# A softcap attention and a mixture-of-experts attention in one kernel: the last pair and batch in an order of their own, logits beside q, projections in pieces, gate weights loaded first

## The chip, the cores and the metric

One core of a Trainium2 chip runs the whole program. Its engines are TensorE (PE, with its weight loads shown apart as PEld), VectorE (DVE), ScalarE (ACT), GpSimd (POOL) and SyncE (SP, which here only issues transfers). The metric is device microseconds of one execution; lower is better.

## What is computed

```python
def _attn_ref(q, k, v, cap):
    scores = scale * np.matmul(q, k.transpose(0, 1, 3, 2))
    scores = cap * np.tanh(scores / cap)
...
    return np.matmul(attn, v).astype(np.float32)

def _moe_ref(x, w_gate, wq, wk, wv, wo):
    logits = x @ w_gate
...
    for e in range(E):
        q = x @ wq[e]
        k = x @ wk[e]
        v = x @ wv[e]
        scores = scale * (q @ k.transpose(0, 2, 1))
...
        ye = a @ v @ wo[e]
        for kk in range(K):
            mask = topk[:, :, kk] == e
            out += mask[..., None] * w[:, :, kk:kk + 1] * ye
```

q, k and v have 8 batches of 12 heads with 448 rows of 64; cap is 30, and the first attention's softmax runs over the last axis. Its output, the 12 heads side by side, is the `x` of the second part (8 x 448 x 768). That has 4 experts of size 64 with causal attention (a is its softmax); each row takes the two experts with the largest logits, weighted by the softmax over these two (w).

## The kernel before

The first attention is worked off in 48 pairs of heads, six to a batch (`NP`, `HP`). For a pair p, ACT does four tanh instructions ("T", on two or one score tiles of 448 columns) and two exps ("E"); the scores come from TensorE into two PSUM tiles of two banks each (`ps_score`). The rest of a pair is casts on POOL (`a_cast`), transposes of q and k (`a_tr`, "tr"), the product with v and the division (`a_pv`, "pv", in two halves) and a transpose of the result into `xT`, the x of the batch (`a_xt`, "xt"). These use four PSUM banks, taken in turn (`ps_aux`).

When the six pairs of a batch b are done, its second part runs beside the pairs of the next batch: q and k projections for two expert pairs r (`b_q`, `b_k`), four v projections with the gate's logits as four more columns of the same matmuls (`b_v`, weights `wvg`), the gate (`b_gate`, `b_gexp`, `b_gate2`), causal scores (`b_fill`) and their exps on ACT ("X", `b_exp`) with masks on POOL, the product with v and the division by DVE (`b_pv`), a transpose (`b_ot`) and eight half-rows of output projection (`b_wo`), which go out by DMA.

`prog` is the order of ACT's work, slot by slot, written by hand; the X of batch b stand in slots 6(b+1)+3 and 6(b+1)+5 (`EXPB`). For TensorE a planner (`Plan`) keeps a clock for PE, DVE and ACT from fixed costs. Each unit of work has a cost, what it depends on, and a due time. `step` takes, among the units that could start first (within 0.05 us), the one due first; `pump` does so up to the next score fill; `force` hurries one unit and what it depends on. Every engine then executes its instructions in the order emitted.

For the last batch the q and k projections are split: `b_early` sums the first five of six steps in score banks once pair 46 is there, one unit for each of q and k and r, and `b_late` adds the sixth. After the last slot, `plan.pump` emits all the rest in the planner's order.

Weights are loaded by POOL's DMA queue (q0 in the page), three loads a slot from slot 1 on, in the order of the list `loads`: wq and wk of the four experts in turn, then the four wv, then the gate's 768 x 4, then wo (line 695 issues them). The inputs q, k, v of two pairs at a time are loaded by SP's queue, eight pairs ahead.

Of the kernel before, what the change touches and what calls it, by code (L numbers as in the profile page):

```python
# [8 lines left out]
f32 = mybir.dt.float32  # L9
# [6 lines left out]
class Plan:  # L16
# [7 lines left out]
    def __init__(self):  # L24
        self.pe = self.dve = self.act = 0.0
        self.done = {}
        self.aux = [0.0] * 4
        self.naux = 0
        self.work = []

    def ready(self, u):
# [5 lines left out]
        if u["aux"]:  # L37
            t = max(t, self.aux[self.naux % 4])
        return t

    def emit(self, u):
# [7 lines left out]
        if u["aux"]:  # L49
            self.aux[self.naux % 4] = end  # L50
            self.naux += 1
        self.done[u["key"]] = end

# [25 lines left out]
    def known(self, key):  # L79
        return key in self.done or any(u["key"] == key for u in self.work)  # L80

    def force(self, key):


        def hurry(k):
            for u in self.work:
                if u["key"] == k:
# [8 lines left out]
    def add(self, key, pe, dve, deps, due, fn, *args, aux=True):  # L96
        self.work.append(
            dict(key=key, pe=pe, dve=dve, deps=deps, aux=aux, due=due, fn=lambda: fn(*args))
        )


@with_exitstack
def kernel(
# [189 lines left out]
    pr = {}  # L293
# [18 lines left out]
    def a_pv(p, i):  # L312

        pv = ps_aux.tile([128, 2, 2, Dh + 1], f32, name=f"pv{i}_{p}", tag="aux")
        pt = (pr[(p, 0)], pr[(p, 1)])
        for n in range(2):
            w = WIN[2 * i + n]
            nc.tensor.matmul(  # L318
                pv[:, n, :, :], pt[0][:, KC, w : w + 128], vtz[p % 8], start=True, stop=False,
                skip_group_check=True,  # L320
            )
            for g in range(2):
                for c in range(KC):
                    nc.tensor.matmul(  # L324
                        pv[:, n, g, :], pt[g][:, c, w : w + 128], v16[p % 8][:, g, c, :],
                        start=False, stop=(c == KC - 1), skip_group_check=True,
                    )
# [9 lines left out]
        )  # L337

# [21 lines left out]
    def b_v(b, n):  # L360
        s = st[b]
        if n == 0:
# [4 lines left out]
        ps = ps_aux.tile([128, E * Dh + E], f32, name=f"vps_{b}_{n}", tag="aux")  # L367
        for j in range(NDC):
            nc.tensor.matmul(  # L369
                ps, xT[b][:, j, w : w + 128], wvg[:, j, :], start=(j == 0), stop=(j == NDC - 1)  # L370
            )
        pse = ps[:, 0 : E * Dh].rearrange("p (e d) -> p e d", d=Dh)
        nc.vector.tensor_copy(s["lg"][:, n, :], ps[:, E * Dh : E * Dh + E])
        if n < 3:
            evac(s["vall"][:, n, :, 0:Dh], pse, act=(b == B - 1))
# [6 lines left out]
    def b_gexp(b):  # L382
        s = st[b]
        s["eexp"] = bp.tile([128, 4, E], f32, name=f"eexp_{b}", tag="eexp")
        nc.scalar.activation(s["eexp"], s["lg"], AF.Exp)

    def b_gate(b):
# [10 lines left out]
        nc.vector.tensor_tensor(mske, lg, m1.broadcast_to(sh), ALU.is_equal)  # L398
# [5 lines left out]
        nc.vector.tensor_tensor(sel, lg, m2.broadcast_to(sh), ALU.is_ge)  # L404
# [19 lines left out]
    def b_qk(b, r, which, ps, j0, j1):  # L424
        w2 = wq2 if which == "q" else wk2
        for j in range(j0, j1):
            nc.tensor.matmul(  # L427
                ps, w2[r][:, j, :], xT[b][:, j, :], start=(j == 0), stop=(j == NDC - 1)
            )
        if j1 < NDC:  # L430
            return
        if which == "q":
            qe = bp.tile([128, S], f16, name=f"qe_{b}_{r}", tag="qe")
            evac(qe, ps, act=(b == B - 1))
            st[b]["qe", r] = qe
            return
# [4 lines left out]
        nc.vector.tensor_copy(kk[64:128, S + TL : 2 * S], ps[64:128, 0:KM])  # L441

    def b_q(b, r):
        ps = ps_aux.tile([128, S], f32, name=f"qps_{b}_{r}", tag="aux")
        b_qk(b, r, "q", ps, 0, NDC)

    def b_k(b, r):
        ps = ps_aux.tile([128, S], f32, name=f"kps_{b}_{r}", tag="aux")
# [385 lines left out]
```

## Time and profile before

| | us |
|---|---|
| median of 3 runs | 356.16 |
| lowest and highest | 352.48 and 358.13 |
| the profiled execution | 357.48 |
| its span in the profile | 355.4 |
| mean granted TensorE clock in it | 0.947 of full speed |

The profile is of one execution on the chip. Times in it are microseconds from the start of the span. A busy time is the sum of an engine's instructions, an idle time is what stood before an instruction, with what ended it after the arrow. The granted clock is 1.0 at 2.4 GHz and 0.5 at 1.2 GHz; a stage's figure is the mean over it.

### The profile page before, as it was taken

To read this page: it belongs to the slowest core of one execution; us is meant where nothing else is said; L and a number is where in the kernel's file an instruction comes from. 1 tells how busy PE (TensorE), PEld (TensorE's weight loads), DVE (VectorE), ACT (ScalarE), POOL (GpSimd) and SP (SyncE) were. 2 spreads that over 40 slices of the span, in tenths; PEclk is the share of its full clock that TensorE was granted. 3 is DMA by queue.
4 is the path that set the end of the run, shared out by engine and by line. 5 is a ranking of instruction groups with operands and counts; after the bars stand their busy time and mean duration, and the time that the engine had idled before them with its cause. 6 is when DMAs were issued, how large, how long until landed. Compare 5 with 4: busy or idle time off the path is not lost.

```text
span 355.4 us, 8921 instructions
## 1 busy us (share of the span) xinstructions
PE 291.3 (82%) x3271; PEld 194.0 (55%) x3271; DVE 251.5 (71%) x881; ACT 308.5 (87%) x340; POOL 164.9 (46%) x527
## 2 busy tenths in 40 slices
PE   4876772897899969997999889988998899896854
PEld 1454441575567556765666656756675656563531
DVE  3366552378778797889678986988688877872382
ACT  1999995499999999999999999999999999971402
POOL 3879999063914383257516480739153602021300
PEclk9599998599999999999999999999999999998678
DMA  5979999930071915374257507670621011100134
GB/s 156 281 189 251 248 227 223 226 93 3 2 243 61 281 39 163 129 222 114 71 176 234 145 9 227 190 201 3 201 92 23 2 46 76 37 2 2 44 111 156
DMA packets 65579, 46.19 MB, mean 130 GB/s; under 512 B 25920, under 2 KB 62400, under 8 KB 65536
## 3 DMA queue, kind: packets, MB, share of 16 engines
q1 hardware_dynamic: 53712, 42.84, 42.1%
q0 software_dynamic: 10512, 1.58, 6.3%
q10 hardware_dynamic: 1312, 1.21, 1.1%
q8 instruction: 25, 0.41, 0.5%
q14 instruction: 18, 0.15, 0.1%
HBM read 36.19 MB, written 11.01 MB: 133 GB/s over the span
## 4 chain that ended last, share of the span: by engine, by line
ACT 69%; DMA 10%; PE 8%; POOL 4%; DVE 3%; SPq 2%; issue 2%; ACTq 0%; POOLq 0%
ACT y L300 31%; ACT p L307 31%; ACT pB L490 7%; DMA wvg<-in_moe_w_gate_dram 4%; DMA kf<-in_k_dram 4%; DMA vf<-in_v_dram 2%; PE vps L369 2%; PE qkps L427 1%; PE wops L551 1%; PE sB L478 1%; POOL wvg L695 1%; DVE osc L528 1%; PE s L289 1%; SPq L165 1%; PE qps L427 1%
## 5 line engine op out<-in xcount | busy, mean ns | idle before, releaser
L300 ACT ACTIVATE y<-s 128x896 f16<-128x896 f32 x192 | 153.3, 885 | 9.9 <-PE s L289 9.8
L307 ACT ACTIVATE p<-y 128x1792 f16<-128x1792 f16 x96 | 150.3, 1567 | 0.0
L498 POOL TENSOR_SCALAR_AFFINE_SELECT pB<-pB 128x128 f16<-128x128 f16 (+1 forms) x128 | 31.9, 280 | 151.1 <-ACT pB L490 150.0
L289 PE MATMUL s<-qt,kz 128*128 128x448 f16 x288 | 82.0, 361 | 17.4 <-ACT y L300 10.4
L324 PE MATMUL pv<-v,p 128*128 128x65 f16 x1152 | 60.0, 194 | 2.4 <-ACT p L307 2.2
L324 PEld LDWEIGHTS <-p 128*128 128x128 f16 x1152 | 51.9, 98 | 8.6 <-ACT p L307 3.5
L289 PEld LDWEIGHTS <-kz 128*128 128x128 f16 x288 | 27.0, 99 | 30.7 <-issue 19.5
L334 DVE TENSOR_TENSOR xk<-pv,rc 128x256 f16<-128x256 f32 x96 | 40.7, 424 | 3.3
L318 PE MATMUL pv<-vtz,p 128*128 128x130 f16 x192 | 42.2, 220 | 0.3
L200 DVE COPY ob<-wops 128x384 f32<-128x384 f32 (+1 forms) x60 | 33.4, 556 | 8.9 <-PE wops L551 7.6
L490 ACT ACTIVATE pB<-sB 128x1024 f16<-128x1024 f32 (+1 forms) x32 | 31.8, 996 | 5.0 <-PE sB L478 5.0
L369 PE MATMUL vps<-wvg,xT 128*128 128x260 f16 x192 | 28.4, 286 | 7.7 <-DMA wvg<-in_moe_w_gate_dram 7.7
L200 DVE COPY kz<-tps 64x384 f16<-64x384 f16 x94 | 32.9, 350 | 0.7
L551 PE MATMUL wops<-wo,oT 128*128 128x384 f16 x128 | 31.9, 341 | 1.1 <-DVE ob L200 0.9
L218 POOL CAST q<-qf 112x512 f16<-112x512 f32 x46 | 28.2, 613 | 2.1 <-DMA qf<-in_q_dram 0.2
L266 DVE COPY qt<-tps 128x384 f16<-128x384 f16 x48 | 16.9, 352 | 16.3 <-PE tps L256 16.2
L369 PEld LDWEIGHTS <-xT 128*128 128x128 f16 x192 | 19.0, 101 | 15.2 <-issue 9.7
L219 POOL CAST k<-kf 128x384 f16<-128x384 f32 x48 | 24.5, 510 | 5.8 <-DMA kf<-in_k_dram 5.8
L235 POOL CAST v<-vf 128x384 f16<-128x384 f32 x48 | 24.3, 507 | 3.2 <-DMA vf<-in_v_dram 0.3
L240 POOL CAST vtz<-vtf 64x64 f16<-64x64 f32 x96 | 22.7, 237 | 2.9
L355 DVE COPY xT<-xtp 128x448 f16<-128x448 f16 x48 | 18.5, 385 | 7.7 <-PE xtp L344 7.3
L333 DVE RECIPROCAL rc<-pv 128x4 f32<-128x4 f32 x96 | 17.2, 179 | 8.9 <-PE pv L324 7.2
(96 smaller groups left out, 487.6 us busy)
## 6 DMA issues: line engine op xcount, KB each, us to landing
qf<-in_q_dram SPq DMA_DIRECT2D x23, 448.0 KB, 4.8
kf<-in_k_dram SPq DMA_DIRECT2D x23, 384.0 KB, 5.3
vf<-in_v_dram SPq DMA_DIRECT2D x23, 384.0 KB, 4.9
out_dram<-ob SPq DMA_DIRECT2D x21, 384.0 KB, 2.4
out_dram<-ob SPq DMA_DIRECT2D x10, 192.0 KB, 2.7
ktf<-in_k_dram SPq DMA_DIRECT2D x46, 32.0 KB, 4.6
vtf<-in_v_dram SPq DMA_DIRECT2D x46, 32.0 KB, 4.2
out_dram<-ob ACTq DMA_DIRECT2D x3, 192.0 KB, 1.9
```

The costliest lines, as they stand in the source:

```text
L200: (nc.scalar.copy if act else nc.vector.tensor_copy)(dst, src)
L218: eng.tensor_copy(q16, qf.rearrange("p h (c d) -> p c h d", c=QC))
L289: nc.tensor.matmul(sc[:, o, 0:S], lhsT, qt, start=True, stop=True)
L300: nc.scalar.activation(y[(p, g)][:, 2 * (i % 2) : 2 * (i % 2) + n, :], score.pop((p, i))[:, 0:n, 0:S], AF.Tanh, scale=isc / capf,)
L307: nc.scalar.activation(pt, y.pop((p, g)), AF.Exp, scale=capf)
L318: nc.tensor.matmul(pv[:, n, :, :], pt[0][:, KC, w : w + 128], vtz[p % 8], start=True, stop=False, skip_group_check=True,)
L324: nc.tensor.matmul(pv[:, n, g, :], pt[g][:, c, w : w + 128], v16[p % 8][:, g, c, :], start=False, stop=(c == KC - 1), skip_group_check=True,)
L334: nc.vector.tensor_tensor(xt[p][:, 2 * i : 2 * i + 2, :, :], pv[:, :, :, 0:Dh], rc.broadcast_to((128, 2, 2, Dh)), ALU.mult,)
L369: nc.tensor.matmul(ps, xT[b][:, j, w : w + 128], wvg[:, j, :], start=(j == 0), stop=(j == NDC - 1))
L490: nc.scalar.activation(pb[:, o0 : o0 + n], st[b].pop(("sc", r, g))[:, 0:n], AF.Exp, scale=isc)
L498: nc.gpsimd.affine_select(out=blk, in_=blk, compare_op=ALU.is_ge, fill=0.0, base=0, pattern=[[1, n]], channel_multiplier=-1,)
L551: nc.tensor.matmul(ps, s["oT", r][:, w : w + 128], wo2[r][:, c0:c1], start=(r == 0), stop=(r == 1))
```

## The change

- The planner can split a unit into parts (`parts`). The first part opens one of the four banks, the last closes it. q and k projections come in three parts of two matmuls, v projections in two of three, the two halves of a pair's product with v in two parts each.
- `loads` starts with the gate weights, issued in slot 0. Then come wq, wk of experts 0 and 1, the four wv, wq, wk of experts 2 and 3, and wo.
- Batch 6's second X pair moves from slot 47 to slot 46. Batch 7's X leave `prog`; slot 47 is four T, then the three remaining E.
- From batch 6 on, due times of the last steps are drawn together (`pace`).
- The last batch's early projections become one unit for each step j, for q and k and both r. The logits of the last batch leave the v projections; 24 matmuls of 4 columns (`b_logit`) sum them in the columns behind q in q's bank.
- `last_batch` writes the order by hand: pair 47's product, head 0 under the last exp and head 1 after it, the transposes, the remaining steps of q, k and logits, then the copies (ACT takes q and a third of k), scores, exps, gate, v projections between the scores, products, and an output projection whose first half (r = 0) for two row blocks is summed before the second product is ready. Three of four output blocks go out as one transfer each.

```diff
@@ class Plan
+    def parts(self, key, n, pe, dve, deps, due, fn, *args):
+        for i in range(n):
+            d = deps if i == 0 else [(*key, "part", i - 1)]
+            aux = "open" if i == 0 else "close" if i == n - 1 else None
+            self.add(
+                (*key, "part", i), pe / n, dve * (i == n - 1), d, due, fn, *args, i, aux=aux,
+                group=key,
+            )
...
+    def b_logit(j0, j1):
+        for j in range(j0, j1):
+            for n in range(4):
+                nc.tensor.matmul(
+                    early[0][:, 0, S + E * n : S + E * (n + 1)],
+                    xT[B - 1][:, j, WIN[n] : WIN[n] + 128], wvg[:, j, E * Dh : E * Dh + E],
+                    start=False, stop=(j == NDC - 1), skip_group_check=True,
+                )
...
-    loads = []
-    for e in range(E):
-        cols = slice(e % 2 * Dh, (e % 2 + 1) * Dh)
-        loads += [(wq2[e // 2][:, :, cols], rows(moe_wq[e]))]
-        loads += [(wk2[e // 2][:, :, cols], rows(moe_wk[e]))]
-    for e in range(E):
-        loads += [(wvg[:, :, e * Dh : (e + 1) * Dh], rows(moe_wv[e]))]
-    loads += [(wvg[:, :, E * Dh : E * Dh + E], rows(moe_w_gate))]
+    loads = [(wvg[:, :, E * Dh : E * Dh + E], rows(moe_w_gate))]
+    for r in range(2):
+        for e in (2 * r, 2 * r + 1):
+            cols = slice(e % 2 * Dh, (e % 2 + 1) * Dh)
+            loads += [(wq2[r][:, :, cols], rows(moe_wq[e])), (wk2[r][:, :, cols], rows(moe_wk[e]))]
+        if r == 0:
+            for e in range(E):
+                loads += [(wvg[:, :, e * Dh : (e + 1) * Dh], rows(moe_wv[e]))]
...
-    EXPB = {HP * (b + 1) + 3 + 2 * r: (b, r) for b in range(B) for r in range(2)}
+    EXPB = {HP * (b + 1) + 3 + 2 * r - (b == B - 2) * r: (b, r) for b in range(B - 1) for r in range(2)}
...
+            prog += t + e1 + [("S", NP), ("E", p, 0), ("E", p, 1)]
...
-        for _ in range(3 if p else 0):
+        for _ in range(3 if p else 1):
...
+            plan.parts(("q", b, r), 3, 1.13, 0.55, [x], t - 4.0, b_qk, b, r, "q")
+            plan.parts(("k", b, r), 3, 1.13, 0.75, [x], t - 4.0, b_qk, b, r, "k")
...
+            plan.parts(("v", b, n), 2, 0.66, 0.6, d, t0 + 2.0 * n, b_v, b, n)
...
+    def last_batch():
...
+        for i in range(2):
+            for n in range(2):
+                do(plan.done["E", p, 0], 0.18, a_pv_mm, p, i, n, (0,))
+        at = [0.0, 0.0]
+        for i in range(2):
+            for n in range(2):
+                at[i] = do(plan.done["E", p, 1], 0.13, a_pv_mm, p, i, n, (1,)) + 0.6
+            a_pv_out(p, i)
...
+        t = do(at[1] + 0.2, 0.22, a_xt, p) + 0.35
+        for r in range(2):
+            for w in "qk":
+                plan.force(("e", r, w, NDC - 2))
+        plan.force(("el", NDC - 2))
...
+        for r in range(2):
+            for w in "qk":
+                t = do(t, 0.19, b_qk_mm, b, r, w, ps[r, w], NDC - 1, NDC)
+            if r == 0:
+                t0 = do(t, 0.18, b_logit, NDC - 1, NDC)
+        for r in range(2):
+            b_q_out(b, r, ps[r, "q"], True)
+            b_k_out(b, r, ps[r, "k"], True)
+            if r == 0:
+                for i in range(2):
+                    do(0.0, 0.33, b_v, b, 0, i)
+                b_gexp(b, lgp)
+                nc.vector.tensor_copy(s["lg"], lgp)
+        for g in range(2):
+            t = do(t0 + 1.1, 0.43, b_fill, b, 0, g)
+            b_exp(b, 0, g)
+        b_gate(b)
+        b_gate2(b)
+        for i in range(2):
+            do(0.0, 0.33, b_v, b, 1, i)
+        t = do(t + 0.4, 0.43, b_fill, b, 1, 0)
+        b_exp(b, 1, 0)
...
+        t = do(t, 0.46, b_pv, b, 0)
+        t = do(t + 0.3, 0.46, b_pv, b, 1) + 0.8
+        do(t, 0.22, b_ot, b, 0)
...
+        b_pv(b, 2)
+        wo(0, (0,))
+        b_pv(b, 3)
+        wo(1, (0,))
+        plan.pump(1.0e9, 1.0e9)
+        b_ot(b, 1)
+        for n in range(2):
+            wo(n, (1,))
+        for n in range(2, 4):
+            wo(n, (0, 1))
```

## Rows read from the trace of the kernel before

**Rows 1.** The page's first part: busy us, share of the span, instructions.

```profile
PE 291.3 (82%) x3271; PEld 194.0 (55%) x3271; DVE 251.5 (71%) x881; ACT 308.5 (87%) x340; POOL 164.9 (46%) x527
```

**Rows 2.** Stages: length, busy time of five engines, granted clock, DMA share, GB/s.

```profile
55.00:75.00 20.00, 11.96 (x112) 8.05 (x109) 7.70 (x27) 10.37 (x12) 8.25 (x28) 0.74 1.00 221
75.00:317.85 242.85, 216.05 (x2616) 149.55 (x2615) 198.45 (x695) 242.85 (x265) 108.34 (x351) 1.00 0.36 109
317.85:326.50 8.65, 6.51 (x58) 3.62 (x57) 3.46 (x9) 0.53 (x1) 0.00 (x0) 0.94 0.01 2
326.50:334.00 7.50, 4.84 (x19) 2.45 (x19) 1.32 (x3) 4.28 (x5) 2.75 (x12) 0.50 0.00 0
```

**Rows 3.** Waits: engine, tile and line, whom for; total us, times, longest.

```profile
ACT y L300 <- PE s L289: 9.8, 4, 7.4
```

**Rows 4.** Timeline, ACT, 57 to 72 us: start, length, instruction, idle before.

```profile
65.48 0.54 ACT L300 ACTIVATE y<-s 128x448 f16<-128x448 f32 x1 [7.35 <-PE s L289]
...
69.62 1.73 ACT L300 ACTIVATE y<-s 128x896 f16<-128x896 f32 x2 [2.02 <-PE s L289]
71.61 1.02 ACT L490 ACTIVATE pB<-sB 128x1024 f16<-128x1024 f32 x1 [0.26 <-PE sB L478]
```

**Rows 5.** Timeline of TensorE's matmuls over the same stretch.

```profile
55.35 0.54 PE L289 MATMUL s<-qt,kz 128*128 128x448 f16 x2 [0.22 <-ACT y L300]
63.61 1.46 PE L369 MATMUL vps<-wvg,xT 128*128 128x260 f16 x6 [7.72 <-DMA wvg<-in_moe_w_gate_dram]
...
66.46 2.44 PE L427 MATMUL qps<-xT,wq 128*128 128x448 f16 x6
```

**Rows 6.** DMA issues of places 11, 12, 13: KB each, us to landing.

```profile
wvg<-in_moe_wv_dram POOLq DMA_DIRECT2D x1, 96.0 KB, 12.6
wvg<-in_moe_wv_dram POOLq DMA_DIRECT2D x1, 96.0 KB, 15.3
wvg<-in_moe_w_gate_dram POOLq DMA_DIRECT2D x1, 6.0 KB, 14.5
```

**Rows 7.** Timeline, POOL: issues of places 10 to 12, then 13.

```profile
43.95 2.46 POOL L695 DMA_DIRECT2D wvg<-in_moe_wv_dram  x3
...
48.98 0.83 POOL L695 DMA_DIRECT2D wvg<-in_moe_w_gate_dram  x1
```

**Rows 8.** The page's DMA queues: POOL's, with packets, MB, share.

```profile
q0 software_dynamic: 10512, 1.58, 6.3%
```

**Rows 9.** The chain that ended last, from 317 us on: start, length, what.

```profile
317.79 0.95 PE qkps L427 x5
...
321.63 0.22 PE xtp L344 x4
...
323.02 0.54 ACT qe L200
...
323.99 0.62 DVE kzB L439
...
324.85 0.49 DVE kzB L441
...
326.51 1.03 ACT pB L490
...
332.85 1.30 PE vps L369 x6
...
336.25 0.67 PE vps L369 x6
...
338.79 0.56 DVE ob L200
...
342.05 0.20 DVE rcB L525
...
342.47 0.42 DVE osc L528
...
347.00 2.43 PE wops L551 x7
```

More of the change, by code (lines that the diff above doesn't have):

```diff
@@ L28, in __init__ @@
         self.naux = 0
+        self.opened = {}
         self.work = []
@@ L36, in ready @@
             t = max(t, self.done[d])
-        if u["aux"]:
+        if u["aux"] in ("open", "whole"):
             t = max(t, self.aux[self.naux % 4])
@@ L48, in emit @@
             end = self.dve + self.LAT
-        if u["aux"]:
-            self.aux[self.naux % 4] = end
+        if u["aux"] in ("open", "whole"):
+            slot = self.naux % 4
             self.naux += 1
+            self.aux[slot] = end
+            if u["aux"] == "open":
+                self.aux[slot] = 1.0e9
+                self.opened[u["group"]] = slot
         self.done[u["key"]] = end
+        if u["aux"] == "close":
+            self.aux[self.opened.pop(u["group"])] = end
+            self.done[u["group"]] = end
     def step(self, until, latest):
@@ L79, in known @@
     def known(self, key):
-        return key in self.done or any(u["key"] == key for u in self.work)
+        return key in self.done or any(key in (u["key"], u["group"]) for u in self.work)
     def force(self, key):
@@ L310, with a_pv_mm, a_pv_out @@
     xt = {}
[L312 to L327, printed above, removed]
+    pvs = {}
+    def a_pv_mm(p, i, n, heads):
+        if n == 0 and 0 in heads:
+            pvs[p, i] = ps_aux.tile([128, 2, 2, Dh + 1], f32, name=f"pv{i}_{p}", tag="aux")
+        pv = pvs[p, i]
+        w = WIN[2 * i + n]
+        for g in heads:
+            pt = pr[(p, g)]
+            if g == 0:
+                nc.tensor.matmul(
+                    pv[:, n, :, :], pt[:, KC, w : w + 128], vtz[p % 8], start=(n == 0),
+                    stop=False, skip_group_check=True,
+                )
+            for c in range(KC):
+                nc.tensor.matmul(
+                    pv[:, n, g, :], pt[:, c, w : w + 128], v16[p % 8][:, g, c, :],
+                    start=False, stop=(c == KC - 1), skip_group_check=True,
+                )
+    def a_pv_out(p, i):
+        pv = pvs.pop((p, i))
         if i == 0:
@@ L539, in b_ot, with b_wo_mm, b_out @@
         s["oT", r] = oT
+    def b_wo_mm(b, n, f, ps, rs):
+        w = WIN[n]
+        for r in rs:
+            nc.tensor.matmul(
+                ps, st[b]["oT", r][:, w : w + 128], wo2[r][:, f * (D // 2) : (f + 1) * (D // 2)],
+                start=(r == 0), stop=(r == 1),
+            )
     def b_wo(b, n, f):
         s = st[b]
-        w = WIN[n]
-        lo = 64 if n == 3 else 0
-        c0, c1 = f * (D // 2), (f + 1) * (D // 2)
         if f == 0:
             s["ob"] = outp.tile([128, D], f32, name=f"ob_{b}_{n}", tag="ob")
-        ob = s["ob"]
         ps = ps_aux.tile([128, D // 2], f32, name=f"wops_{b}_{n}_{f}", tag="aux")
-        for r in range(2):
-            nc.tensor.matmul(
-                ps, s["oT", r][:, w : w + 128], wo2[r][:, c0:c1], start=(r == 0), stop=(r == 1)
-            )
+        b_wo_mm(b, n, f, ps, (0, 1))
+        b_out(b, n, f, ps)
+    def b_out(b, n, f, ps):
+        lo = 64 if n == 3 else 0
+        w = WIN[n]
+        c0, c1 = f * (D // 2), (f + 1) * (D // 2)
+        ob = st[b]["ob"]
         last = b == B - 1
         evac(ob[lo:128, c0:c1], ps[lo:128, :], act=last and f == 1)
-        if last:
+        if last and n == 3:
             eng = nc.sync if f == 0 else nc.scalar
```

195 lines of the change are left out of this document (114 added, 81 removed).

## Prediction

> **What bounds the kernel now.** I read the page's first part first, to see which engine can set the time: ACT is busy 87% of the span, and no other engine over 82% [rows 1]. An average says little here, so the stages came next. Between 75.00 and 317.85 us ACT is busy for 242.85 of 242.85 us [rows 2]: the middle of the kernel is a string of tanh and exp without a gap, and nothing that only rearranges other engines can shorten it. What can be won lies in two places: the 20 us before 75.00, of which ACT works 10.37, and the 37.55 us after 317.85, where the attention pairs are over and the last batch drains.
>
> The list of waits names the first place: ACT waited for TensorE's scores, 9.8 us in 4 waits, the longest 7.4 [rows 3]. In order of time, ACT sits idle 7.35, 2.02 and 0.26 us, 9.63 in all, between 58.1 (65.48 less 7.35) and 71.6 [rows 4]. TensorE's side shows why: the scores at 55.35 are followed by nothing until the first v projection of batch 0 starts at 63.61, after 7.72 us of waiting for the gate weights [rows 5]. TensorE takes its work in order, so the scores behind that projection wait too. Its first work after the hole is slow: six q matmuls take 2.44 us, against 0.95 for five late in the kernel [rows 5, 9]. The granted clock over the stage is 0.74, a mixture of both levels, after an engine that stood still for over 7 us [rows 2]. Part of the second idle time, 2.02 us, is this.
>
> The chain of work from 317 us on shows the second place [rows 9]. The last exp of pair 47 ends at 317.85 [rows 2], the first exp of batch 7 starts at 326.51, the first division of its attention at 342.05, its last output projection at 347.00, and the span ends at 355.40. That is 8.66 + 15.54 + 4.95 + 8.40 = 37.55 us of one thing after another.
>
> **The change, step by step: gate weights first.** Before, POOL issues the gate load at 48.98 as the 13th of 17 [rows 7] and it lands 14.5 us later, at 63.5, where TensorE goes on [rows 6, 5]. After, it is issued right after pair 4's casts, near 24, and batch 0 needs it at about 55.9: far ahead. What is late next? The wv loads move from places 9 to 12 of the big loads to 5 to 8, so they land before 50. But wq and wk of experts 2 and 3 now take places 9 to 12. The loads that held places 11 and 12 were issued at about 44.8 and 45.6 and took 12.6 and 15.3 us [rows 6, 7], landing at 57.4 and 60.9. POOL issues each 0.83 us later, since the gate load's own 0.83 us [rows 7] now lies ahead of them: 58.2 and 61.7. The first is wq of expert 3, the second wk of expert 3. TensorE wants q of the second expert pair right behind the first v projection: in the old order only one score tile, two sets of transposes and then that q stand there [rows 5], so at about 57 without the hole. ACT has work until 58.1 [rows 4], so a wait until 58.2 costs it under a microsecond. The k of that pair stood behind the v projections before. As smaller pieces it can slip between them, and would then wait up to 61.7. I take 2.1 us of ACT idle time for both together and a gain of 7.5. The bounds are 9.63 (no wait) and 3.0 (TensorE blocked from 57 to 61.7, and then as much recovery as the 2.3 us seen now, which makes near 7 lost).
>
> **Projections in pieces, weights' order, one exp pair moved.** Cutting q, k, v and the attention products into pieces adds no matmul; it lets the planner fill smaller gaps. In the middle this is worth nothing, because ACT has no idle time there [rows 2]. The cover is ACT itself; if a piece opened a bank and blocked TensorE, ACT would lose it directly (a rival, below). Batch 6's second expert pair moves one slot earlier, out of the last one. It is the same ACT work, but the last slot then has four tanhs in a row with no exp between, so the third must wait for scores whose bank is released one tanh earlier. I put 0.5 us on that, between 0 and one score fill with its latencies, about 1.
>
> **From the last exp to the first exp of batch 7 (8.66 us).** Now four runs of five early projections stand in TensorE's order behind the last exp, 0.95 us each [rows 9]. After, single steps are emitted as soon as each transposed pair is there, so most of this runs during the last slot, and half of pair 47's product runs under the last exp. I build the path: 0.6 for the second half of the product, 1.3 for two divisions (0.20 and 0.42 each, by the like operations of [rows 9], with latencies), 0.8 for four transposes and their copy (0.22 and 0.4): the last projection step starts at 2.7 after the exp, and ACT's copy of q at 3.1, which now starts at 323.02, 5.2 after it. Now k is projected only after that copy, and then three DVE copies follow, from 323.99 to 325.34 [rows 9]. After, k follows q at once, and ACT takes the third copy: k is ready at about 4.1 instead of 7.5. Then a cost that the change adds: the logits share q's bank, so the bank is free for the scores only when the logits are copied out, and that copy stands on DVE behind the first v evacuation: I put that at 5.1. Scores at full clock 0.5: first exp at 5.7, saving 2.9. The logits' own 24 matmuls of 4 columns, no dearer than the 0.055 us of a transpose (four in 0.22 [rows 9]), are 1.3 us, five sixths of it before the path.
>
> **From the first exp to the first division (15.54 us).** Now a second late projection, four v projections, batch 6's output projections and the nine gate operations stand in one line. Six v matmuls cost 1.30 us at clock 0.5 and 0.67 at full clock [rows 9]; the stage's first half ran at 0.50 [rows 2]. After, both projections come ahead of the scores, the gate runs on DVE under the exps, and the v projections stand between score fills. What stays is ACT: four exps of about 0.95 [rows 9] and two copies of at most 0.5, some 4.5 to 4.8, and about 1.0 for the last v copy and the first product. I take 5.5, saving 10.0. If TensorE ran at the low level throughout, three v's and three fills would add some 3 us.
>
> **The rest.** The division-to-output stage keeps its order of divisions, and its first transposes hold up the next products: 5.2 against 4.95. Behind it, half of the output sums are made beforehand, and three outputs go as one transfer each instead of two: 7.5 against 8.40, most of it copies and the transfer's landing, which don't shrink. Sum 5.7 + 5.5 + 5.2 + 7.5 = 23.9. Against it stand leftovers of batch 6: eight output copies of 0.56 on DVE [rows 9], which ran in the tail before and, as TensorE was already 89% busy in the middle [rows 2] and now gets the early projections there, partly will again. Three of them on the path are 1.6: 25.5 in place of 37.55, a saving of 12.0, with bounds 7.5 (low clock and all leftovers) and 14.
>
> **Sum.** 357.48 (the profiled execution; its span is 355.4, so 2.1 lie around it) - 7.5 + 0.5 - 12.0 = 338.5. That execution stands 1.3 above the median of the runs; I say 338.
>
> **Rivals.**
> *The wait moves to the second pair's weights.* For it: their loads take the very places that landed at 57.4 and 60.9. The gate load has as many pieces as a big one: 10512 packets on that queue [rows 8] are 13 loads of 784 and 4 of 80, so it counts with 784. If pieces rather than bytes set the pace, putting it first pushes all others back by the 2.6 us by which it landed after its predecessor (63.5 less 60.9), to 60.8 and 64.3. TensorE then stalls as now, the gain is about 2.5, and the time 357.48 - 2.5 + 0.5 - 12.0 = 343.5. Against it: k stood late in the old order. The Trainium skill's page "DMA: Bandwidth & Descriptors" (Why small descriptors are slow) gives such a rule: the engine pays a fixed overhead for each packet. By it this rival is the likelier; the trace agrees in so far as 6 KB took about as long as 96 KB [rows 6].
> *The tail gives half back.* Gaps remain while DVE divides, and TensorE fell to clock 0.5 after gaps of this kind [rows 2]; with all leftovers the saving is 7: time 343.5. For it: DVE's copies of 0.56 sit between divisions now [rows 9]. Against: the new order has more to do in each gap.
> *Everything lands.* 9.63 and 14: 334.
> *Banks held open block the middle; slower than before.* An open piecewise sum holds one of four banks until its last piece is done; with two or three open, the running pair's products wait for a bank, TensorE stands, and ACT follows. DVE, which frees them, is 82% busy (198.45 of 242.85 [rows 2]). The cost falls on seven batches: at 2.8 us of ACT idle time a batch the gain of 19 is gone, at 3.8 the kernel is over 2% slower, about 365. Against: ACT has zero idle time there now with whole projections.
>
> **Chances.** Forecast 0.50; weights 0.22; tail 0.13; everything 0.07; blocked middle 0.04; smaller mishaps that leave it within 2% 0.04. About 2% is what a measurement tells from no change. Faster by over 2% holds for the first four: 0.92; within 2% 0.06; slower 0.02. The range takes the bounds: 334 for all gains less the 1.3 of the profiled execution, so 332 in round numbers, up to 347 (gains of 3.0 and 7.5); beyond it lie about 0.15.
>
> **What would show it.** The wait on the gate weights gone, ACT's idle time between 55 and 75 down from 9.6 to about 2, and what is left put down to projections of the second pair. ACT still without idle time from there to the last exp, which ends near 311. From it to the first exp of batch 7 5.7 us, to the first division 5.5 more, to the end of the span 25.5 in all, with the early projections ahead of the last exp. Wrong would be idle time on ACT in the middle, another wait of 4 us or more on a weight load near 57, or a granted clock of 0.5 through most of the last 25 us.

## The result, and the profile after

| | before | after |
|---|---|---|
| median, us | 355.24 | 340.15 |
| lowest and highest | 352.48 and 358.13 | 339.57 and 342.68 |
| the profiled execution, its span | 357.48, 355.4 | 342.68, 341.0 |
| granted clock in it | 0.947 | 0.989 |

The ratio is 0.9614, with a 95% interval of 0.9526 to 0.9702: faster, by 3.9%. It compares the means of the fast runs, 340.64 after and 354.32 before, where the run of 358.13 counts as slow and is left out. The forecast was 338 with a range of 332 to 347. The total came out close, but two of its terms did not: the tail gave 8.3 us in place of 12.0, and the head, in nine of ten traces with the new loads and pieces, gave 9.6 in place of 7.5. That they partly cancel is luck.

The page's first part, and the waits of ACT (engine, tile and line, whom for; total us, times, longest), after:

```profile
PE 280.2 (82%) x3295; PEld 190.1 (56%) x3295; DVE 251.1 (74%) x877; ACT 308.4 (90%) x341; POOL 165.2 (48%) x527
...
ACT ob L223 <- DVE ob L223: 8.2, 1, 8.2
...
ACT qe L223 <- PE qkps L506: 6.0, 1, 6.0
ACT pB L540 <- PE sB L528: 2.4, 1, 2.4
ACT y L323 <- PE s L312: 1.9, 4, 1.0
```

ACT's own work is what it was [rows 1]: 308.4 us. Only idle time around it went. The wait of 9.8 us for scores [rows 3] is down to 1.9. Of the waits left, two long ones belong to the tail: 6.0 us for the first copy of q, and 8.2 at the very end.

Stages of after: length, busy time of five engines, granted clock, DMA share, GB/s. They answer to [rows 2]:

```profile
55.00:75.00 20.00, 16.36 (x178) 11.37 (x177) 12.24 (x44) 16.18 (x18) 13.29 (x43) 0.91 0.89 205
75.00:308.00 233.00, 206.84 (x2496) 143.30 (x2496) 190.41 (x660) 233.00 (x256) 103.23 (x335) 1.00 0.39 115
```

Between 55 and 75 us ACT works 16.18 us in place of 10.37. In the middle it has no gap, either before or after. The last exp of pair 47 ends at 311.76 (307.58 and 4.18 in the row below); before, at 317.85.

The tail of after, from ACT's timeline (start, length, instruction, idle before and what ended it):

```profile
307.58 4.18 ACT L330 ACTIVATE p<-y 128x1344 f16<-128x1344 f16 x3
317.77 0.53 ACT L223 CAST qe<-qkps 128x448 f16<-128x448 f32 x1 [6.02 <-PE qkps L506]
319.23 0.47 ACT L223 CAST kzB<-qkps 64x384 f16<-64x384 f32 x1 [0.92 <-DVE kzB L483]
321.75 1.89 ACT L540 ACTIVATE pB<-sB 128x1024 f16<-128x1024 f32 x2
```

and from its chain of work (start, us, what), answering to [rows 9]:

```profile
325.84 0.20 DVE rcB L575
...
332.54 2.71 DMA out_dram<-ob
```

So the tail's stages are 9.99 us from last exp to first exp of batch 7 (311.76 to 321.75), 4.09 to the first division (325.84), and 15.16 to the end (341.0): 29.24. Before they were 8.66, 15.54 and 13.35: 37.55. The whole gain lies in the middle one; the first and the third grew.

The account of the two profiled executions: ACT's idle time from 50 to 80 us fell from 9.63 to 3.81 (5.82), the rest up to the last exp was 0.27 shorter, the tail 8.31, and what lies around the span 0.4 (2.1 against 1.7). That is 14.8, the difference of 357.48 and 342.68.

### The profile page after: what moved, and what is told of

Its sections match the earlier page's. It is cut to its first block, busy times and chain, and to the rows that moved or that the text cites. A ratio compares the mean times of both kernels' runs of the same rounds, so it can differ in the third digit from the quotient of the medians.

```text
span 341.0 us, 8954 instructions
## 1 busy us (share of the span) xinstructions
PE 280.2 (82%) x3295; PEld 190.1 (56%) x3295; DVE 251.1 (74%) x877; ACT 308.4 (90%) x341; POOL 165.2 (48%) x527
## 4 chain that ended last, share of the span: by engine, by line
ACT 85%; PE 6%; DMA 2%; issue 2%; DVE 2%; POOL 1%; ACTq 0%; POOLq 0%
ACT y L323 39%; ACT p L330 37%; ACT pB L540 7%; POOL pB L548 1%; DMA kf<-in_k_dram 1%; PE qkps L469 1%; PE vps L407 1%; PE s L312 1%; DMA out_dram<-ob 1%; PE sB L528 1%; DMA vtf<-in_v_dram 1%; DVE ob L223 1%; PE qps L469 0%; PE pv L351 0%; ACT L223 0%
## 5 line engine op out<-in xcount | busy, mean ns | idle before, releaser
L351 PE MATMUL pv<-v,p 128*128 128x65 f16 x1152 | 66.2, 194 | 1.2 <-ACT p L330 1.0
L351 PEld LDWEIGHTS <-p 128*128 128x128 f16 x1152 | 53.7, 98 | 11.0 <-ACT p L330 2.0
L312 PEld LDWEIGHTS <-kz 128*128 128x128 f16 x288 | 26.2, 98 | 26.4 <-issue 13.1
L379 PE MATMUL xtp<-perm,xk 128*128 128x128 f16 x144 | 21.0, 223 | 14.4 <-DVE xk L364 14.2
L594 PE MATMUL wops<-wo,oT 128*128 128x384 f16 x128 | 29.8, 325 | 1.7 <-DVE oT L588 1.7
L407 PE MATMUL vps<-wvg,xT 128*128 128x260 f16 (+1 forms) x192 | 30.6, 276 | 0.0
L379 PEld LDWEIGHTS <-xk 128*128 128x128 f16 x192 | 14.6, 98 | 27.3 <-DVE xk L364 19.1
L289 DVE COPY qt<-tps 128x384 f16<-128x384 f16 x48 | 16.9, 352 | 15.2 <-PE tps L279 14.8
```

Source lines behind the costliest of these rows:

```text
L312: nc.tensor.matmul(sc[:, o, 0:S], lhsT, qt, start=True, stop=True)
L351: nc.tensor.matmul(pv[:, n, g, :], pt[:, c, w : w + 128], v16[p % 8][:, g, c, :], start=False, stop=(c == KC - 1), skip_group_check=True,)
L379: nc.tensor.transpose(ps[:, 128 * n : 128 * (n + 1)], src(n), first if n < 3 else last)
L407: nc.tensor.matmul(ps, xT[b][:, j, w : w + 128], wvg[:, j, 0:cols], start=(j == 0), stop=(j == NDC - 1),)
L594: nc.tensor.matmul(ps, st[b]["oT", r][:, w : w + 128], wo2[r][:, f * (D // 2) : (f + 1) * (D // 2)], start=(r == 0), stop=(r == 1),)
```

## The experiments

One table first, from each kernel's trace, in us. "Idle" is ACT's idle time from 50 to 80 us; A is the end of the last exp of pair 47; then the way from A to ACT's first copy of q, on from there to the first exp of batch 7 (X), to the first division (D), and to the end of the span. The medians are of the timed runs, the ratios against runs of the kernel before that were timed beside them. Each trace is of one execution.

| kernel | idle | A | A to q copy | q copy to X | X to D | D to end | median | ratio and 95% interval |
|---|---|---|---|---|---|---|---|---|
| before | 9.63 | 317.85 | 5.17 | 3.49 | 15.54 | 13.35 | 355.24 | |
| after | 3.81 | 311.76 | 6.01 | 3.98 | 4.09 | 15.16 | 340.15 | 0.9614 [0.9526, 0.9702] |
| e1 | 0.70 | 309.85 | 5.16 | 3.07 | 15.22 | 13.40 | 351.82 | 0.9802 [0.9716, 0.9888] |
| e2 | 10.68 | 318.74 | 6.02 | 3.97 | 5.61 | 15.06 | 351.31 | 0.9795 [0.9716, 0.9873] |
| e3 | 0.00 | 312.43 | 6.02 | 3.97 | 5.76 | 15.12 | 343.46 | 0.9590 [0.9518, 0.9662] |
| e4 | 0.00 | 308.07 | 7.26 | 3.97 | 5.76 | 15.14 | 341.91 | 0.9636 [0.9568, 0.9704] |
| e5 | 0.00 | 308.68 | 6.24 | 3.32 | 4.08 | 15.18 | 340.41 | 0.9586 [0.9515, 0.9656] |
| e6 | 0.00 | 307.47 | 6.01 | 3.97 | 5.76 | 13.89 | 339.56 | 0.9568 [0.9493, 0.9643] |
| e7 | 0.52 | 312.15 | 6.43 | 3.97 | 4.09 | 15.16 | 348.10 | 0.9687 [0.9591, 0.9782] |
| e8 | 0.00 | 308.86 | 5.21 | 3.91 | 6.41 | 16.71 | 343.25 | 0.9681 [0.9587, 0.9776] |
| e9 | 0.00 | 308.03 | 6.32 | 3.96 | 4.10 | 16.89 | 341.49 | 0.9597 [0.9529, 0.9665] |
| e10 | 0.00 | 307.67 | 6.02 | 3.96 | 4.10 | 14.55 | 338.26 | 0.9511 [0.9449, 0.9573] |
| e11 | 0.00 | 308.81 | 6.03 | 3.97 | 4.09 | 15.20 | 340.21 | 0.9550 [0.9485, 0.9615] |
| f2 | 0.00 | 308.72 | 6.76 | 3.32 | 4.08 | 13.42 | 338.19 | 0.9498 [0.9453, 0.9542] |

### e1: the loads alone

```diff
 # kernel before
-    loads = []        # wq, wk of four experts, four wv, the gate
+    loads = [gate]    # then wq, wk of 0 and 1, four wv, wq, wk of 2 and 3
-        for _ in range(3 if p else 0):
+        for _ in range(3 if p else 1):
```

> The kernel before with the new order of weight loads alone. If the parts simply add, the head's share is what ACT's idle time between 55 and 75 us loses: from 9.6 us to about 4 to 5, so the time falls by 5 to 6, to about 350, and the 37.6 us behind the last exp stay as they were. Rival: the wait only moves to the second expert pair's weights in full, because the old order asks for that q right behind the first v projection, as one unit of six matmuls: then ACT's idle time stays at 7 or more and the time falls by under 3.

### e2: all of the change but the loads

```diff
 # kernel after
-    loads = [gate]    # the new list
+    loads = []        # the list of before
-        for _ in range(3 if p else 1):
+        for _ in range(3 if p else 0):
```

> The changed kernel with the old order of loads: the gate weights are 13th again. If the wait on them is a matter of the loads alone, TensorE stands still until they land, at about 63, some 8 to 9 us because the first v projection now comes earlier (54.3), ACT is idle some 9 to 10 us there, and the time is 5 to 6 us over that of the changed kernel, 345 to 346. Rival: the pieces make room for other work before the first v projection and soften the wait: then under 3 us over it.

The load order alone gives 2.0%, the rest alone 2.05%, and together they give 3.9%: the two gains add up as far as intervals of some 0.9% either way can tell, and neither alone is clear of 2%. In e2 the hole of [rows 5] is back, a little longer than expected (9.81 us of TensorE, 10.68 of ACT). TensorE's and ACT's timelines of e2:

```profile
64.07 0.81 PE L407 MATMUL vps<-wvg,xT 128*128 128x260 f16 x3 [9.81 <-DMA wvg<-in_moe_w_gate_dram]
...
66.84 1.36 ACT L323 ACTIVATE y<-s 128x896 f16<-128x896 f32 x2 [9.77 <-PE s L312]
```

The gate weights cause it, whatever the shape of the projections. In e1, with whole projections, the hole shrinks to one wait of TensorE, for the load that the forecast called late next. ACT's idle time falls to 0.70 us, not to the 4 to 5 expected; but the traced execution, 348.73, is the shortest of e1's four, and the others (351.42 to 354.31) are not traced.

```profile
59.91 1.30 PE L427 MATMUL qps<-xT,wq 128*128 128x448 f16 x6 [0.92 <-DMA wq<-in_moe_wq_dram]
```

### e3: four loads in slot 0

```diff
-        for _ in range(3 if p else 1):
+        for _ in range(3 if p else 4):
```

> The changed kernel with four weight loads in slot 0 instead of one, so that each load behind them is issued a slot, some 5 us, sooner. Theory: what is left of the head's wait (TensorE 2.7 us before the q of the second expert pair, ACT 3.8 us in all) ends when the wq of expert 3 lands. Then the wait and the idle time are gone and the last exp ends 3 to 4 us earlier; the time falls by 3. Rival: the queue moves at its own pace and sooner issues only wait in it: the landing moves by under 1 us, and so does the time. Second rival: POOL's 2.5 us of issuing in slot 0 delay the casts of pairs 5 and 6, and ACT waits near 30 to 45 us instead.

In after's own profile wq of expert 3 landed late. POOL issued it at 45.17 and it took 19.0 us, so it landed near 64.1; TensorE goes on at 64.22. Issues and the DMA list (last column: us to landing), then TensorE's and ACT's timelines, all of after:

```profile
23.67 0.97 POOL L746 DMA_DIRECT2D wvg<-in_moe_w_gate_dram  x1 [0.24 <-issue]
45.17 0.83 POOL L746 DMA_DIRECT2D wq<-in_moe_wq_dram  x1
...
wq<-in_moe_wq_dram POOLq DMA_DIRECT2D x1, 96.0 KB, 19.0
...
64.22 0.91 PE L469 MATMUL qps<-xT,wq 128*128 128x448 f16 x2 [2.69 <-issue]
...
65.96 0.97 ACT L540 ACTIVATE pB<-sB 128x960 f16<-128x960 f32 x1 [2.39 <-PE sB L528]
67.36 0.92 ACT L323 ACTIVATE y<-s 128x896 f16<-128x896 f32 x1 [0.42 <-PE s L312]
69.28 0.54 ACT L323 ACTIVATE y<-s 128x448 f16<-128x448 f32 x1 [1.00 <-PE s L312]
```

The trace labels the 2.69 us "issue"; that they are a wait for wq is read from the landing and 64.22. Three more loads in slot 0 did not bring this one forward: it is issued at 44.88 instead of 45.17. POOL paces the issues, among its casts. The wait at 60 is gone in e3, but then it is also gone in most kernels here with the new order, so that is not the edit's doing. What the edit does is early, and it is the second rival. ACT stands idle 2.35, 1.64 and 0.67 us between 22 and 35. The first of these ends before a load is issued, so the edit is not its cause. The other two, 2.31 us, follow the four loads: the cast of the next q stands behind them, and TensorE waits for it. POOL's, TensorE's and ACT's timelines of e3:

```profile
25.95 0.97 POOL L746 DMA_DIRECT2D wvg<-in_moe_w_gate_dram  x1 [1.01 <-issue]
...
30.38 0.37 PE L272 MATMUL tps<-ident,q 112*128 112x112 f16 x4 [1.64 <-POOL q L241]
...
25.20 1.35 ACT L323 ACTIVATE y<-s 128x896 f16<-128x896 f32 x2 [2.35 <-PE s L312]
...
32.61 0.92 ACT L323 ACTIVATE y<-s 128x896 f16<-128x896 f32 x1 [1.64 <-PE s L312]
```

### e11: the gate load fifth, none in slot 0

```diff
-    loads = [gate]    # then wq, wk of 0 and 1, ...
+    loads = []        # wq, wk of 0 and 1, then the gate, ...
-        for _ in range(3 if p else 1):
+        for _ in range(3 if p else 0):
```

> The changed kernel with the gate load as fifth instead of first, in slot 2, and nothing issued in slot 0. Theory: the 0.97 us that its issue takes on POOL in slot 0 delay the casts of pair 5 and what follows, and this is why ACT idles 0 to 1.8 us between 20 and 50 us in the runs with the new order, and 0.05 before: without it that idle time is under 0.3. The wait for the weights of the second expert pair may come back, since their loads leave a little later: 0 to 2 us near 62. Rival: the early idle time has another cause, the loads of k, and stays.

It is as fast as after (340.21 against 340.15). The load need not be first: fifth, behind four long ones, it still lands near 41, and ACT has no idle time near 62. ACT's idle time from 20 to 50 us is 0.69 here, not under 0.3, and lies between 0 and 1.8 in the kernels with one load in slot 0, so that load isn't shown to cause it; its cause stays open.

### e7: projections whole

```diff
     def parts(self, key, n, pe, dve, deps, due, fn, *args):
-        for i in range(n):
-            ...
+        def whole():
+            for i in range(n):
+                fn(*args, i)
+        self.add(key, pe, dve, deps, due, whole)
```

> The changed kernel with q, k, v projections and the products with v emitted as whole units again, all else kept. Theory: the pieces are worth nothing in the middle, where ACT has no idle time: ACT stays without idle time from 75 us to the last exp, and the time is within 1 us of the changed kernel. Rival A: the pieces keep TensorE ahead, and whole units cost ACT 0.5 us or more a batch, 3 us in all. Rival B: the pieces brought the second expert pair's q forward into the wait for its weights: whole units then save 1 to 3 us in the head.

With whole units the new loads and the new tail still hold. But the middle is no longer without gaps: 1.90 us in four waits of 0.47 to 0.48, near 156, 195, 233 and 271 us, one batch (38 us) apart. The first, on ACT's timeline, and TensorE's wait in the head:

```profile
156.37 0.54 ACT L321 ACTIVATE y<-s 128x448 f16<-128x448 f32 x1 [0.47 <-PE s L310]
...
59.45 1.29 PE L467 MATMUL qps<-xT,wq 128*128 128x448 f16 x6 [0.70 <-DMA wq<-in_moe_wq_dram]
```

So in this trace the pieces are worth about 1.9 us in the middle, nearer to rival A than to the theory. They also bring TensorE to q of the second pair at 61.3 to 62.7 us (66.1 in e3) instead of 59 or so; the load is then there in nine of ten kernels. The median is 348.1, with runs at 350.5, 347.91 and 348.29 beside the profiled one of 343.76. Why these are 4 to 7 us longer no trace here shows, so the pieces may be worth more than 1.9; it stays open.

### e4: the early projections ahead of everything

```diff
-            due = nom["S", NP] + 1.0
+            due = nom["S", NP] - 12.0
```

> The changed kernel with the last batch's early projections and logits due 13 us sooner, so that they go ahead of batch 6's products and output projections. Theory: 15 of the 20 early steps stood behind the last exp only because that other work was due first; with them ahead, the first copy of q starts 2 to 3 us sooner after the last exp (6.0 now), and the time falls by 1 to 2, part of it lost to the work that is put off. Rival: TensorE is simply full in the last slot, and what is pushed back lands on the tail just as long: no change within 1 us.

The tail's first stage was the largest miss, so the next runs went there. TensorE's part of the chain of after, from 312 us on, and its stages (as above, first the length, then PE) show where the 6.0 us before q's copy go:

```profile
312.36 0.94 PE qkps L469 x5
...
314.93 0.22 PE xtp L379 x4
...
316.98 0.28 PE qkps L506 x12
...
317.77 0.54 ACT qe L223
```

```profile
312.00:314.00 2.00, 1.96 (x29) 1.26 (x26) 1.40 (x6) 0.00 (x0) 0.00 (x0) 1.00 0.00 0
314.00:316.00 2.00, 2.00 (x18) 1.20 (x17) 1.26 (x5) 0.00 (x0) 0.00 (x0) 1.00 0.03 8
316.00:318.00 2.00, 2.00 (x30) 1.30 (x29) 0.93 (x2) 0.23 (x1) 0.00 (x0) 1.00 0.00 0
```

TensorE is busy 5.96 of 6.00 us. Fifteen of the twenty early steps still stand behind the last exp, and so do the transposes of pair 46. Asking for the early steps sooner left eight of them there and made it worse: 7.26, as what they pushed back (pair 46's products and transposes among it) comes before q's last step too. TensorE is then busy 6.51 of the 7.26 us and waits, for DVE above all, in the rest.

```profile
315.33 0.53 ACT L223 CAST qe<-qkps 128x448 f16<-128x448 f32 x1 [7.26 <-PE qkps L506]
```

### e9: batch 6's output last

```diff
     # batch 6's products and output projections
-    due = t1 + pace * (...)
+    due = t1 + pace * (...) + 100.0
```

> The changed kernel with batch 6's products and output projections due 100 us later, so that they yield to everything of pair 46, pair 47 and the early projections. Theory: TensorE is full from the last scores to the first copy of q, and of what stands there four products, two transposes and two output projections of batch 6 (some 2.7 us) need not; without them the copy of q starts 1.5 to 2.5 us sooner after the last exp than 6.0. What is put off then stands between the divisions later: the time falls by 0 to 1.5. Rival: the chain of pairs 46 and 47 through DVE (division, transposes, copy) sets that copy, not TensorE's load: it starts less than 0.5 us sooner, and the time rises by what was put off, 1 to 3.

A due time alone does not keep batch 6 out of the stretch: two of its products and both of its transposes, which in after ran before the last exp, now stand behind it, and seven early steps went ahead in exchange. TensorE is busy 5.41 of 6.3 us, no longer full, and the chain runs over DVE, where two of batch 6's divisions stand ahead of TensorE's last steps (chain of e9: start, us, what):

```profile
310.57 0.42 DVE xk L364
...
311.31 0.42 DVE osc L578
...
312.06 0.43 DVE osc L578
...
312.54 0.40 PE otp L379 x4
```

So it came out as the rival said: the copy starts no sooner (6.32), the end grows to 16.89, and the median is 1.3 above after's. As ordered there, the path through DVE takes as long as TensorE's load does in after. With e4 and f2 below, three orders gave 6.3 to 7.3: none tried beat after's 6.0. What the stage takes with batch 6 wholly out of it was not run.

### e8: the logits back in the v projections

```diff
-        cols = E * Dh if b == B - 1 else E * Dh + E
+        cols = E * Dh + E
...
-                plan.add(("el", j), 0.18, 0.0, d, due + 2, b_logit, j, j + 1, aux=None)
```

> The changed kernel with the last batch's logits back in its v projections (260 columns), and exp and gate behind the fourth of them; the 24 small matmuls are gone. Theory: the gate's nine DVE operations, about 2 us, then stand between the last v projection and the first division: the time rises by 1.5 to 2. Rival: the logits cost the front as much as they save behind, since they share q's tile and add an exp and a copy to the chain of copies there: no change within 1 us.

```profile
314.07 0.53 ACT L223 CAST qe<-qkps 128x448 f16<-128x448 f32 x1 [5.21 <-PE qkps L468]
```

The copy of q comes 0.80 us sooner than in after (5.21 against 6.01). The 24 small matmuls are 0.53 of that in after's chain (0.08, 0.08, 0.28 and 0.09), 0.022 each and below the 0.055 of the forecast; much of the rest is an output projection of batch 6 (0.35), which in e8 comes later. From X to D they earn 2.32 (6.41 against 4.09), as the gate no longer stands behind the v projections. The last stage is 1.55 shorter in after (15.16 against 16.71), but that is not the gate alone: the granted clock was 0.56 for three us of e8's last stage, and e8 has that output projection left. The net of 3.0 us in the tail (32.24 against 29.24) is thus an upper figure for this part of the change.

### e5: q and k in tiles of their own

```diff
-            early[r] = ps_score.tile([128, 2, 512], f32, name=f"qkps_{r}", tag="score")
+            early[which] = ps_score.tile([128, 2, 512], f32, name=f"{which}ps", tag="score")
...
-                d = [..., ("T", NP-1, 2 + r)]
+                d = [..., ("T", NP-1, 2 if w == "q" else 3)]
```

> The changed kernel with both q sums in one tile of two banks and both k sums in the other, in place of q and k of one expert pair together. Theory: ACT's copy of q and DVE's copies of k took turns (0.5, 0.9, 0.5 us one behind the other) because they read the same tile; apart they overlap, and the first exp of batch 7 comes about 1.2 us sooner after the first copy of q (4.0 now); the time falls by about 1. Rival: they take turns for another reason, and nothing moves.

From q's copy to the first exp after takes 3.98 us: its chain goes ACT qe, two DVE copies, ACT's third copy, and then the same again for r = 1, before the exp at 321.75. ACT does in order what the program gives it, so the second set of copies stands ahead of the first exp. With q's and k's sums apart, ACT's wait for DVE shrinks from 0.92 to 0.60, and the stage to 3.32: 0.66 sooner, half of the 1.2 expected.

```profile
316.05 0.47 ACT L223 CAST kzB<-kps 64x384 f16<-64x384 f32 x1 [0.60 <-DVE kzB L483]
```

The total gain is 0.43 from A to X, and the medians can't tell the kernels apart (340.41 and 340.15).

### e6: batch 6's leftover copies on ACT

```diff
-        act=(last and f == 1)
+        act=(last and f == 1) or (b == B - 2 and tail[0])
     def last_batch():
+        tail[0] = True
```

> The changed kernel with those output copies of batch 6 that are emitted after the last slot made by ACT instead of DVE. Theory: they stand in DVE's way between the divisions (0.56 and 0.56) and ahead of the last copy of the transposed product (four, 2.1 us), and the late transfer of the last of them holds the buffer that the last output block needs; without them the stage from first division to end, 15.2 us, shrinks by 2 to 3, and the time by as much. Rival: the final transfers set the end by their bandwidth: under 1 us.

DVE's timeline of after shows what the last stage grew by:

```profile
326.60 0.55 DVE L223 COPY ob<-wops 128x384 f32<-128x384 f32 x1
...
327.81 0.55 DVE L223 COPY ob<-wops 128x384 f32<-128x384 f32 x1
...
330.44 2.08 DVE L223 COPY ob<-wops 128x384 f32<-128x384 f32 x4
332.54 0.39 DVE L588 COPY oT<-otp 128x448 f16<-128x448 f16 x1
```

Six copies of output rows stand among the divisions, four of them just before the copy of the transposed product that the final output projection needs. With those of batch 6 on ACT, which is idle there, the stage is 13.89 instead of 15.16, a gain of 1.3 and not 2 to 3. The last copy still ends 10.0 us after the first division (10.1 in after), since now it waits for a buffer, as the chain of e6 says:

```profile
328.14 3.78 DMA out_dram<-ob
```

### e10: e6 and eight output buffers

```diff
-    tc.tile_pool(name="outp", bufs=4)
+    tc.tile_pool(name="outp", bufs=8)
```

> The kernel with the leftovers' copies on ACT, and eight buffers instead of four for output rows. Theory: with ACT copying, the end was held only by the buffer of the last block, which waited 3.8 us for batch 6's last transfer; with its own buffer the stage from the first division to the end, 13.9 us there and 15.2 in the changed kernel, falls to about 11 and the time by 2 to 3 against either. Rival: the transfers still set the end, since SP sends them in turn: under 1 us.

Now no copy waits for a transfer: the last one ends at 330.43, 8.7 us after the first division (10.1 in after). Part of this gain of 1.4 doesn't arrive. The end of the span is at 336.3, 5.9 us after the last copy (5.1 in after), since more transfers now share those microseconds. The DMA list of e10 from 320 us on (count, KB each, us to landing), and a stage in which only the DMA is busy, with a share of 0.99:

```profile
out_dram<-ob SPq DMA_DIRECT2D x5, 384.0 KB, 3.2
...
out_dram<-ob ACTq DMA_DIRECT2D x1, 96.0 KB, 4.7
out_dram<-ob SPq DMA_DIRECT2D x1, 96.0 KB, 4.6
...
332.00:334.00 2.00, 0.00 (x0) 0.00 (x0) 0.00 (x0) 0.00 (x0) 0.00 (x0) 1.00 0.99 319
```

In after a copy waited until 335.25 for a transfer that took 2.71; in e10 the two last transfers of 96 KB take 4.6 and 4.7 (4.0 and 3.5 in after), behind larger ones. D to end is 14.55, as the rival said. The median, 338.26, lies 1.9 below after's, with intervals that overlap.

### f2: e5 and e10, and pair 46 ahead

```diff
 # e5 and e10, and in last_batch
+        plan.force(("xt", p - 1))    # before pair 47's product, head 0
+        plan.force(("el", NDC - 2))  # before head 1
```

> Three edits read at three places: pair 46 is finished (second half of its product, transposes) and its logit steps are summed before pair 47's second half, q sums and k sums have a tile each, and leftovers go over ACT with eight output buffers. Theory: in the changed kernel the last projection steps waited for pair 46, whose second half had come behind pair 47's; with it first the copy of q starts 4.5 after the last exp instead of 6.0. Rival: TensorE's load alone sets it, and it stays at 5.7 or more. From that copy to the first exp of batch 7 3.3 instead of 4.0, as with the tiles alone, and from the first division to the end 14.5 instead of 15.2. In all 338.3 less 1.5 to 2, near 336.5; by the rival 337.5 or more.

It is the lowest median, 338.19, ratio 0.9498 [0.9453, 0.9542]. Its tail is 27.58 against 29.24. The first stage isn't what improved: 6.76 to q's copy, above the rival's 5.7, and 10.08 to X against 9.99. The end is (13.42); which of the edits does that, beyond e10's 14.55, wasn't taken apart. Against after the intervals still touch, so "better than after" is likely and not shown; against the kernel before it is 5.0%.

## Why the prediction was right, and where its terms were not

**The gate weights (7.5 said).** The wait on them is gone, as said: the load was issued at 23.67 as forecast ("near 24"), and lands far ahead. What is late next was named rightly too: wq of expert 3. Its landing was put at 58.2; it was 59.45 and 59.91 where TensorE stood waiting for it (e7, e1), near 64.1 in after's profile, and 57.3 to 62.5 in the others with this order. The price of it was wrong in both directions. In after's own profile the idle time is 3.81 instead of 2.1, so the stage gave 5.82. In the nine other profiles with the new order and pieces (e3 to e6, e8 to e11, f2) it is 0.00, so the stage gives 9.63, the upper bound. The step that failed is that TensorE wants that q at about 57: with whole projections it asks for it near 59 (e1, e7), and with pieces of other work ahead at 61.3 to 62.7. After's profile is the one of ten in which the load came later than that and ACT paid; it is also the longest of after's four runs. In f2 the load came 0.1 us before TensorE took it, so the margin is small, and how often ACT pays isn't shown. (The forecast's lower bound is its own sum rounded up: 4.7 and 2.3 lost of 9.63 leave 2.6, not 3.0.)

**The last slot (0.5 said).** ACT works without a gap in it. A less the idle time from 50 to 80 us is 308.22 in the kernel before and 307.95 in after: the four tanhs in a row cost nothing that shows.

**The middle (nothing said).** True of the change: ACT has no gap in either kernel, and "banks held open", the rival on the other side, found nothing. But the pieces are not without effect there. e7 has 1.90 us of waits without them, which the kernel before did not have, so with the rest of the change they hold off a loss, of that size or more.

**Last exp to first exp (5.7 said, 9.99 found).** This is the term that failed, in two steps.
- q's copy was to start 3.1 after the exp; it starts 6.0 after it. The path to it was built of latencies, and TensorE taken to be free for them, with most early steps run in the last slot. It was busy 5.96 of 6.00 us, with 15 of 20 early steps, pair 46's transposes and all 24 logit matmuls, of which five sixths were to come before. TensorE was 89% busy in the middle [rows 2]; there was little room to take them. The three other orders tried (e4, e9, f2) didn't help, and e9 shows DVE's chain right behind as the next bound. The forecast drew that very conclusion for batch 6's leftovers, but not for these steps.
- From there to the exp 2.6 were said, 3.98 found. The copies do alternate between ACT and DVE, and the set for r = 1 stands on ACT ahead of the first exp. The logits' copy, which the forecast took for the gate of this stage, is not what the chain shows; e5 is worth 0.66 here.

**First exp to first division (5.5 said, 4.09 found).** The mechanism was right and the size too careful: 15.54 became 4.09, the one place where the whole tail gain lies. (The forecast's 0.95 us for an exp is not in [rows 9], where the one exp shown takes 1.03.) e8 puts 2.32 of it down to the logits. Where the granted clock fell in this stage it took 5.6 to 5.8 (e2, e3, e4, e6).

**The rest (5.2 + 7.5 + 1.6 = 14.3 said, 15.16 found).** The leftovers were seen, but they are six copies on DVE and not three, and behind them a buffer waits 2.71 for a transfer. e6 and e10 together show why taking them away gives 0.6 of the 1.6: the copies then end 1.4 sooner, and the transfers that follow take 0.8 longer.

**The sum.** The tail gave 8.31 instead of 12.0, and the head 5.82 in this profile and 9.6 in others. The profiled execution is 342.68 against the 338.5 of the sum; the median is 2.15 above the 338 that was said. So the forecast held by its mechanism at the head and from X to D, and by luck in the sum, where the head's surplus makes up for half of what the tail lacks. Of the rivals, "the tail gives half back" is the nearest to what happened (its 7 against 8.31). The leftovers that it counts on did come; the rest has another cause: neither gaps of TensorE nor the low clock, but TensorE without any gap.

**The rule on small descriptors.** The rule of the Trainium skill's page "DMA: Bandwidth & Descriptors" (Why small descriptors are slow) is a fixed overhead for each packet. As the forecast read it, the gate load, put first, would have pushed the others back by 2.6 us. It took 14.5 us in the old order [rows 6] and 3.9 in the new (DMA list of after):

```profile
wvg<-in_moe_w_gate_dram POOLq DMA_DIRECT2D x1, 6.0 KB, 3.9
```

The same 784 pieces, a quarter of the time: most of the 14.5 was not the pieces' own, and what was ahead on the queue is the likely rest. The trace does not contradict a cost for each piece, but its size here is at most these 3.9 us, paid when nothing waits.

## What to carry to other kernels

Ahead of a path built out of latencies, add up all the work of the engine that it runs on, in that stretch: if that is as long as the stretch, a new order of the same work can do little, as three tries here show. Then look for the next longest path, on another engine, before taking work away. A wait removed at the head and one at the tail of a kernel whose middle is full add up, and can be forecast one by one. Where copies are taken off the end, look at the transfers behind them before counting the gain.

## What the runs showed of the hardware that was not expected

The granted clock fell in some executions and not in others after like activity. Three stretches of 2 us from 6 us after the last exp on, first after, then e6 (length, busy times of PE, PEld, DVE, ACT and POOL, granted clock, DMA share, GB/s):

```profile
317.76:319.76 2.00, 1.03 (x8) 0.58 (x6) 1.27 (x3) 1.05 (x3) 0.00 (x0) 1.00 0.50 197
319.76:321.76 2.00, 0.61 (x4) 0.34 (x5) 1.47 (x6) 1.05 (x4) 0.00 (x0) 1.00 0.00 0
321.76:323.76 2.00, 1.99 (x18) 1.61 (x18) 1.19 (x7) 2.00 (x3) 0.92 (x4) 1.00 0.00 0
```

```profile
313.47:315.47 2.00, 1.03 (x8) 0.58 (x6) 1.27 (x3) 1.05 (x3) 0.00 (x0) 1.00 0.50 197
315.47:317.47 2.00, 0.61 (x4) 0.34 (x5) 1.47 (x6) 1.05 (x4) 0.00 (x0) 1.00 0.00 0
317.47:319.47 2.00, 2.00 (x11) 1.37 (x11) 1.18 (x7) 1.95 (x3) 0.93 (x4) 0.61 0.00 0
```

The first two stretches are alike to the hundredth in both. Then after stays at 2.4 GHz, and e6 goes to a mixture near the 1.2 GHz level and does 11 matmuls where after does 18. It costs 1.7 us (5.76 against 4.09 from X to D). What decides between the two is open.

The same load from the same place in the order landed 13 us after its issue in e1 and e7 and 19.0 in after (wq of expert 3, 96 KB). From 40 to 65 us all queues together moved 226 GB/s in after, 260 in e1 and 246 in e10; why less in after isn't shown. It is worth up to 3.8 us of ACT's time.
